# Chunked attention into a phase MLP on one core: the first group's q and k on SyncE's queue in fp32, theta on the load queue, and another written order

## The chip, the cores and the metric

The kernel runs on one NeuronCore of a Trainium2 chip. The metric is the device time of one execution in microseconds (us); smaller is better. The engines are named as in the profile: PE (TensorE; PEld is its weight load), DVE (VectorE), ACT (ScalarE), POOL (GpSimd) and SP (SyncE). POOL and SP issue DMAs, and so does ACT.

## The reference

Attention inside chunks of 64 tokens, for 8 batches, 8 heads, 576 tokens and a head width of 64; its output, with the heads side by side, is the input x (8 x 576 x 512) of an MLP layer:

```python
scores = scale * q_c @ k_c^T            # per chunk of 64, softmax over the chunk
x      = softmax(scores) @ v_c          # (B, S, 512)
theta  = x @ w_theta
y      = w_tok_r @ (x * cos(theta)) + w_tok_i @ (x * sin(theta))   # over tokens
u      = x + y
out    = u + max(u @ w_ch, 0)
```

All inputs and the output are fp32. The kernel works in fp16 with fp32 sums.

## The kernel before, in words

The 8 batches are worked off as 4 pairs (p = 0 to 3). The 1152 tokens of a pair are cut into five groups: A and B are 256 tokens each of the first batch, C and D of the second, and M holds the last 64 tokens of both. A step of the kernel is one stage for one group, and for some steps one half of it (the digit behind the letter).

Nothing is scheduled by a tool at run time: the text ORDER (line 16) lists every step, and the loop at the end emits them in that order (lines 769 to 782), so each engine executes its instructions in the order in which they stand there. A step is written `kind.pairgroup.bank`; `S1.0A.2` is the scores of the second half of group A of pair 0 into PSUM bank 2. The kinds that matter here are:

- `q`, `k` (line 173): load of a group's q or k by POOL's queue, which casts fp32 to fp16 on the way. It has two layouts. In the usual one two tokens lie in one partition, so that a packet reads 512 bytes; in the plain one (`qP`, `kP`) one token does, two DMAs are issued, and a packet reads 256 bytes. `v` (line 205) issues three DMAs for a group, two for M. `lw`, `lc` and `lt` load the weights; `lt` (line 240) brings theta in fp32 by SP's queue and `ctV` casts it on DVE.
- `L`, `T`, `N` (line 285): transposes of q and k on PE, in three forms. `T` (small) takes 64 transposes of 64x64 for a group, `L` (long) 32 of 64 to 128 wide, `N` (plain, needed for a plain load) 16 of 128x128. `tq`, `tkA`, `tkV` (line 328) copy the results out of PSUM, q by DVE and k by ACT or DVE.
- `S`, `e`, `V`, `n`: scores on PE, exp on ACT, product with v on PE, normalisation on DVE, which gives x.
- `X`/`Q`, `xA`/`xV`: transposes of x on PE (128x128, or small ones of 64x64) and their copy by ACT or DVE. `H`: product with theta (line 479), `g`: cos and sin on ACT, `z`: their products with x on DVE.
- `TW`, `twV`: transposes of the token weights and their copies. `Y`, `K`: the product over tokens (lines 551, 565, 654). Pair 0 takes it straight (`Y`); the pairs 1 to 3 take a form with fewer products (`K`), with sums of z (`j`) on DVE.
- `U`/`R`, `uA`/`uV`, `W`, `w`, `s`/`sA`: transposes of u, their copies, the product with w_ch, the relu and sum on DVE, and the store by SP's (`s`) or ACT's (`sA`) queue.
- `D.n`: n dummy matmuls of 128x512 on zeros (line 276), which need only the memset of `init` (line 131).

Three things hold loads back. For the pairs 1 to 3 a load step first copies one element of the newest normaliser on POOL (`gate`, line 167), so that POOL waits until DVE got there. The tiles of q, k, token weights, sums of z and the late outputs share one pool of ten buffers (`nat`, line 105), so that a load waits until the tile ten allocations earlier was read for the last time. And POOL's loads use eight semaphores in turn, so that the ninth waits for the first to land. PSUM's eight banks are given out by hand in ORDER.

Of the kernel before, what the change touches and what calls it, by code (L numbers as in the profile page):

```python
# [9 lines left out]
FP32 = mybir.dt.float32  # L10
FP16 = mybir.dt.float16
# [2 lines left out]


ORDER = """
lt.00 init.00 id.00 D.12.0 ctV1.00 q.0A k.0A D.19.0 L0.0A.0.1 tq0.0A q.0C L1.0A.2.3 tq1.0A k.0C
v.0A tkA1.0A S1.0A.2 L.0C.0.4 tq.0C tkA0.0A S0.0A.6 e1.0A tkA.0C q.0B k.0B e0.0A ctV0.00 D.3.0
V0.0A.0 V1.0A.2 n1.0A S.0C.6 e.0C q.0M n0.0A L0.0B.7.6 L1.0B.5.4 X0.0A.0 tkA0.0B tq0.0B k.0M
N1.0M.1 v.0B N0.0M.2 tq1.0B tkA1.0B S1.0B.6 tq1.0M tq0.0M X1.0A.3 xA0.0A e1.0B S0.0B.4 e0.0B  # L20
tkV1.0M S1.0M.0 e1.0M v.0C V1.0B.6 xV1.0A tkV0.0M n1.0B S0.0M.2 e0.0M V0.0B.4 n0.0B H0.0A.0
V0.0C.6 n0.0C pg.00 g0.0A V1.0C.2 v.0M X1.0B.1 xV1.0B H1.0A.4 q.0D g1.0A X0.0B.7 V0.0M.6 V1.0M.1
H1.0B.5 g1.0B n1.0C X.0C.0 xV0.0B k.0D L.0D.7.2 tkA.0D n0.0M n1.0M X.0M.1 z0.0A xV.0M lw.00
tq.0D z1.0A H0.0B.3 H.0M.1 S.0D.4 g0.0B xV.0C TW.01.6 TW.00.2 g.0M lw.02 e.0D twV.01 v.0D H.0C.0
q.1B twV.00 YA.0A.2 k.1B q.1A V0.0D.4 z1.0B z0.0B V1.0D.6 z.0M YB.0A.2 YM.0A.2 g.0C TW.02.0
n1.0D TW.03.6 twA.02 n0.0D Q.0D.4 y.0A T.1B.2 R.0A.0 lc.00 twV.03 YA.0B.6 xA.0D uA.0A jw.00
jw.01 H.0D.0 tkA.1B g.0D tq.1B z.0C k.1A S.1B.4 T.1A.2 tq.1A YM.0B.6 q.1D YB.0B.6 tkA.1A W.0A.0
q.2A k.2A T.2A.2 y.0B e.1B tkA.2A k.1D T.1D.6 tkA.1D z.0D YD.0C.4 tq.2A YC.0C.4 S.1A.2 q.1M e.1A
w.0A q.1C k.1C k.1M T.1C.0 v.1B tq.1D S.1D.6 tq.1C YM.0C.4 v.1C YD.0D.2 YM.0D.2 e.1D y.0C
V0.1B.4 tkA.1C lw.04 V1.1B.0 v.1A sA.0A n0.1B S.1C.6 e.1C n1.1B YC.0D.2 y.0D X.1B.0 TW.04.1  # L30
twV.04 N.1M.7 tq.1M xA.1B S.2A.4 e.2A V0.1A.2 v.1D v.1M q.3B V1.1A.0 Y.0M.6 n1.1A n0.1A tkA.1M
V0.1C.0 S.1M.2 y.0M e.1M k.3B V1.1C.4 n1.1C U.0D.7 X.1A.6 v.2A n0.1C uA.0D xV.1A H.1B.2 V0.1D.0
pg.00 g.1B V1.1D.4 n1.1D H.1A.6 q.2M V0.1M.5 g.1A n0.1D n0.1M V1.1M.4 n1.1M z.1B Q.1C.0 xA.1C
q.2C k.2C W.0D.2 U.0B.4 V0.2A.6 uA.0B w.0D v.2B X.1D.5 n0.2A H.1C.0 T.3B.6 V1.2A.2 xA.1D H.1D.4
q.2D z.1A g.1C g.1D tq.3B v.2D v.2M W.0B.0 n1.2A Ka.1A.2 v.3A z.1C tkA.3B Q.1M.4 ja.1C w.0B
T.2C.6 Q.2A.0 ra.1A xA.1M H.1M.4 U.0C.5 xA.2A tq.2C z.1D tkA.2C k.2M H.2A.0 g.1M q.2B k.2B jb.1D
Ke.1C.6 z.1M v.3B re.1D Kf.1C.2 rc.1C uA.0C W.0C.4 w.0C Kc.1D.6 T.2B.4 g.2A sA.0D jc.1D jd.1B
S.2C.0 pe.00 e.2C tq.2B tkA.2B rd.1C Kg.1D.2 rg.1B Kd.1B.0 rh.1B v.2C S.2B.4 e.2B q.3C Km.1D.2
U.1C.7 uA.1C S.3B.0 k.3C rf.1D V1.2C.4 k.2D Y.1M.6 T.2D.2 q.3M n1.2C e.3B sA.0C y.1M tkA.2D
V0.2C.0 n0.2C V1.2B.4 U.1B.7 uA.1B tq.2D N.2M.6 U.0M.0 uA.0M X.2C.1 xA.2C tq.2M Kb.1B.2 tkA.2M  # L40
S.2D.0 n1.2B s.0B V0.2B.4 z.2A W.1B.6 rb.1A n0.2B e.2D V0.2D.0 n0.2D S.2M.2 w.1B H.2C.4 V1.2D.0
e.2M v.3M W.0M.2 U.1A.3 n1.2D V0.2M.0 w.0M Q.2B.6 n0.2M V1.2M.1 n1.2M X.2D.2 pg.00 g.2C z.2C
W.1C.4 xA.2D w.1C H.2D.0 xA.2B uA.1A V0.3B.2 q.3A s.0M ja.2C n0.3B g.2D Q.2M.6 xV.2M H.2B.4 g.2B
R.1M.2 uV.1M V1.3B.0 T.3C.6 H.2M.2 g.2M U.1D.3 uA.1D n1.3B z.2D tq.3C jb.2D tkA.3C s.1B Ka.2A.0
s.1C k.3M ra.2A v.3C Ke.2C.4 jc.2D Q.3B.2 xA.3B S.3C.6 e.3C z.2M q.3D Kf.2C.0 rc.2C W.1D.2 k.3D
k.3A w.1D z.2B H.3B.6 pg.00 g.3B re.2D Kg.2D.0 rg.2B T.3D.2 tkA.3D W.1A.6 tq.3D v.3D Km.2D.0
w.1A Kc.2D.4 S.3D.2 rf.2D rd.2C pe.00 e.3D T.3A.0 Kb.2B.6 tq.3A jd.2B N.3M.2 rb.2A sA.1D tkA.3A
S.3A.0 tkA.3M V1.3D.4 Y.2M.3 tq.3M S.3M.6 n1.3D e.3A V0.3A.4 y.2M V0.3D.0 W.1M.2 U.2A.3 n0.3D
e.3M n0.3A uA.2A X.3D.0 xA.3D V0.3M.1 w.1M V1.3A.6 n1.3A Kd.2B.4 X.3A.0 n0.3M rh.2B V0.3C.6
V1.3M.1 H.3D.2 xA.3A n1.3M n0.3C Q.3M.0 pg.00 g.3D xV.3M V1.3C.4 n1.3C H.3A.6 z.3B Q.3C.0 xV.3C  # L50
R.2B.4 W.2A.2 z.3D w.2A g.3A z.3A uA.2B H.3M.0 H.3C.6 g.3M z.3M R.2D.0 g.3C R.2C.2 W.2B.4 z.3C
ja.3C Kb.3B.6 rb.3A jb.3D uA.2C W.2C.2 uA.2D w.2C sA.2A Ka.3A.6 ra.3A W.2D.0 Ke.3C.2 Kf.3C.6
sA.2C sA.1A w.2B re.3D jc.3D rc.3C Kc.3D.2 R.3A.4 Kg.3D.6 s.2B rd.3C uA.3A W.3A.2 jd.3B Kd.3B.4
rg.3B w.2D s.2D w.3A Km.3D.6 R.3C.0 uA.3C rh.3B Y.3M.2 rf.3D s.1M R.3B.0 uV.3B sA.3A R.3D.6
W.3C.4 y.3M uA.3D W.3D.6 w.3C U.3M.0 W.3B.4 w.3D uV.3M sA.3C w.3B R.2M.0 sA.3D s.3B W.3M.2 uA.2M
W.2M.0 w.3M sA.3M w.2M sA.2M
""".split()


# [1 line left out]
def kernel(  # L61
# [11 lines left out]
    nc = tc.nc  # L73
    B, H, S, D = q.shape
    DM = H * D
    CH = 64
    P = 128
    NDB = DM // P
    NE = H // 2
# [4 lines left out]
    GT = 2 * P  # L84
# [5 lines left out]
    GROUPS = {  # L90
        "M": (MID, None, KT * P),
        "A": (0, 0, 0),
        "B": (2, 0, GT),
        "C": (5, 1, 0),
        "D": (7, 1, GT),
    }
# [8 lines left out]
    nat = ctx.enter_context(tc.tile_pool(name="nat", bufs=10))  # L105
# [16 lines left out]
    wtheta16 = glob.tile([P, NDB, DM], FP16, name="wtheta16")  # L122
# [1 line left out]
    wT = glob.tile([P, NK, S], FP16, name="wT")  # L124
    wsum = [glob.tile([P, 2, 2, GT], FP16, name=f"wsum{i}") for i in range(4)]
    v16 = glob.tile([P, 2 * NT, H, VP], FP16, name="v16")
    wraw = []
    wnat = {}

    def setup():  # L130
# [9 lines left out]
    st = {p: {} for p in range(NP)}  # L140
# [23 lines left out]
    nats = {}  # L164
    marks = []

    def gate(p):

        if p and marks:
            nc.gpsimd.tensor_copy(out=seen, in_=marks.pop())  # L170
            marks.clear()

    def load_qk(p, g, which, plain, f=None):
# [28 lines left out]
            ),  # L202
        )

    def load_v(p, g):

        gate(p)
        j0, bb, s0 = GROUPS[g]
        slot = (p % 2) * NT + j0
        if bb is None:  # L210
            for b in range(2):
                nc.gpsimd.dma_start(
                    v16[half[b], slot, :, 0:D],
                    v[2 * p + b, :, s0 : s0 + CH, :].rearrange("h s d -> s h d"),
                )
            return
        for rows, tile, t0, m in (
            (slice(0, P), 0, s0, P),
            (half[1], 1, s0 + P, CH),
            (half[0], 1, s0 + P + CH, CH),  # L220
        ):
            nc.gpsimd.dma_start(  # L222
                v16[rows, slot + tile, :, 0:D],
                v[2 * p + bb, :, t0 : t0 + m, :].rearrange("h s d -> s h d"),
            )
# [12 lines left out]
                wnat.setdefault(i + j, []).append(t[:, j])  # L238

    def load_theta():  # L240
        for a in range(2):
            t = nat.tile([P, 2, DM], FP32, name="wraw", tag="nat")
            wraw.append(t)
            nc.sync.dma_start(
                t, moe_w_theta[a * GT : a * GT + GT, :].rearrange("(a p) e -> p a e", p=P)
            )

    def cast_theta(a, copy):
        copy(out=wtheta16[:, 2 * a : 2 * a + 2], in_=wraw[a])

    def load_w_ch():
        nc.gpsimd.dma_start(wch16, moe_w_ch.rearrange("(a p) e -> p a e", p=P))
# [75 lines left out]
    def qk_copy(p, g, f, which, how):  # L328
        ps = st[p]["ps_qkT", g, f][which]
        _, nx, n, c = ps.shape  # L330
        name = "qk"[which] + "T"
        t = tmp.tile([P, nx, n, c], FP16, name=name, tag=f"{name}{n}")
        st[p][name, g, f] = t
        if how == "V":
            nc.vector.tensor_copy(out=t, in_=ps)  # L335
        elif n == 1 or st[p]["form", g, f] == "plain":
            nc.scalar.copy(out=t, in_=ps)
        else:
            nc.scalar.copy(  # L339
                out=t.rearrange("p x s c -> p x (s c)").rearrange(  # L340
                    "p x (c s) -> p x c s", s=2
                ),
                in_=ps.rearrange("p x s c -> p x c s"),
            )
# [355 lines left out]
    def store(p, g, f, queue):  # L700
# [12 lines left out]

    work = {
        "v": load_v,
        "lt": lambda p, g: load_theta(),
        "id": lambda p, g: make_identity(nc, id16),
# [17 lines left out]
        "k": lambda p, g, f: load_qk(p, g, 1, False, f),  # L735
        "qP": lambda p, g, f: load_qk(p, g, 0, True, f),
        "kP": lambda p, g, f: load_qk(p, g, 1, True, f),
        "ctA": lambda p, g, f: cast_theta(f, nc.scalar.copy),
        "ctV": lambda p, g, f: cast_theta(f, nc.vector.tensor_copy),
        "T": lambda p, g, f, *banks: qk_t(p, g, f, "small", *banks),  # L740
        "L": lambda p, g, f, *banks: qk_t(p, g, f, "long", *banks),
        "N": lambda p, g, f, *banks: qk_t(p, g, f, "plain", *banks),
        "tq": lambda p, g, f: qk_copy(p, g, f, 0, "V"),
        "tkV": lambda p, g, f: qk_copy(p, g, f, 1, "V"),
        "tkA": lambda p, g, f: qk_copy(p, g, f, 1, "A"),
        "S": scores,
# [22 lines left out]
    with tc.manual_schedule():  # L769
        for step in ORDER:  # L770
# [5 lines left out]
            p, g = int(at[0]), int(at[1]) if at[1].isdigit() else at[1]  # L776
# [36 lines left out]
```

## Time and profile before

| what | value |
|---|---|
| three timed executions | 206.13, 206.96, 207.36 us; median 206.96 |
| the profiled execution, its own time | 207.38 us |
| its span in the trace | 205.5 us |
| PE busy | 190.5 us (93%) |
| DVE, ACT, POOL busy | 153.8, 118.1, 88.5 us |
| mean granted PE clock | 0.981 |
| bytes moved by DMA packets | 26.99 MB, 16.01 of them by POOL's queue |

The profile is taken from one execution. The span runs from the program's first to its last instruction. Busy time counts what an engine executes, and for PE it includes the dummies. The table of windows gives the same busy times for stretches of the span, with the granted clock and the DMA traffic in each. The chain of waits starts at the last instruction and goes back, at each step, to what released it. A line of the groups shows the kind, the shapes, how often it ran, its busy time in us and its mean in ns.

### The profile page before, as it was taken

To read this page: it belongs to the slowest core of one execution; us is meant where nothing else is said; L and a number is where in the kernel's file an instruction comes from. 1 tells how busy PE (TensorE), PEld (TensorE's weight loads), DVE (VectorE), ACT (ScalarE), POOL (GpSimd) and SP (SyncE) were. 2 spreads that over 40 slices of the span, in tenths; PEclk is the share of its full clock that TensorE was granted. 3 is DMA by queue.
4 is the path that set the end of the run, shared out by engine and by line. 5 is a ranking of instruction groups with operands and counts; after the bars stand their busy time and mean duration, and the time that the engine had idled before them with its cause. 6 is when DMAs were issued, how large, how long until landed. Compare 5 with 4: busy or idle time off the path is not lost.

```text
span 205.5 us, 7697 instructions
## 1 busy us (share of the span) xinstructions
PE 190.5 (93%) x3472; PEld 102.5 (50%) x3472; DVE 153.8 (75%) x246; ACT 118.1 (57%) x139; POOL 88.5 (43%) x129
## 2 busy tenths in 40 slices
PE   7975999999669999999799999999999999999990
PEld 2454565464444755454456455454566444444540
DVE  0144678895436879997877898989988998799670
ACT  2065769778516598877157588888446983010310
POOL 8959983297761968889530040870000000000000
PEclk9999589999999999999999999999999999999998
DMA  6999999999993999999993059999200011613456
GB/s 210 170 171 149 103 186 178 192 162 174 167 129 111 82 151 88 166 200 200 157 168 113 3 55 197 142 134 99 100 5 3 3 38 69 243 67 115 143 219 189
DMA packets 86832, 26.99 MB, mean 131 GB/s; under 512 B 80016, under 2 KB 81680, under 8 KB 86800
## 3 DMA queue, kind: packets, MB, share of 16 engines
q0 software_dynamic: 81264, 16.01, 92.9%
q10 hardware_dynamic: 3040, 5.77, 7.9%
q1 hardware_dynamic: 2496, 4.72, 6.7%
q8 instruction: 27, 0.44, 0.9%
q14 instruction: 5, 0.04, 0.1%
HBM read 33.06 MB, written 9.44 MB: 207 GB/s over the span
## 4 chain that ended last, share of the span: by engine, by line
PE 80%; DMA 11%; POOL 3%; issue 2%; DVE 0%; POOLq 0%; DVEq 0%
PE ps L479 30%; PE ps L654 18%; PE ps L565 8%; DMA qk<-in_k_dram 7%; PE ps L439 5%; DMA v<-in_v_dram 4%; PE ps L551 4%; PE ps L401 3%; PE ps L319 3%; PE ps L367 3%; PE ps L448 3%; POOL qk L198 2%; PE ps L267 2%; PE ps L302 1%; POOL qk L184 1%
## 5 line engine op out<-in xcount | busy, mean ns | idle before, releaser
L222 POOL DMA_DIRECT2D v<-in_v_dram x48 | 36.4, 779 | 4.4 <-DMA qk<-in_k_dram 1.7
L479 PE MATMUL ps<-wtheta,xT 128*128 128x512 f16 x144 | 35.8, 390 | 0.0
L479 PE MATMUL ps<-wch,uT 128*128 128x512 f16 x144 | 34.1, 380 | 0.0
L673 DVE TENSOR_TENSOR x<-ps,x 128x1024 f16<-128x1024 f32 x24 | 29.1, 1222 | 5.7 <-PE ps L654 5.1
L462 ACT COPY uT<-ps 128x1024 f16<-128x1024 f16 (+1 forms) x17 | 16.2, 968 | 25.0 <-PE ps L448 17.5
L383 ACT ACTIVATE eT<-ps 128x1024 f16<-128x1024 f32 (+1 forms) x18 | 16.6, 930 | 19.0 <-PE ps L367 19.0
L415 DVE TENSOR_TENSOR x<-ps,recip 128x512 f16<-128x512 f32 (+1 forms) x40 | 25.5, 638 | 1.4
L339 ACT COPY kT<-ps 128x1024 f16<-128x1024 f16 (+1 forms) x18 | 16.4, 921 | 16.4 <-PE ps L306 11.9
L335 DVE COPY qT<-ps 128x1024 f16<-128x1024 f16 (+2 forms) x23 | 13.0, 572 | 16.5 <-PE ps L306 5.9
L493 ACT ACTIVATE cos<-ps,pihalf 128x1024 f16<-128x1024 f32 (+1 forms) x22 | 21.1, 959 | 7.3 <-PE ps L479 7.2
L694 DVE SCALAR_TENSOR_TENSOR o<-ps,x 128x1024 f32<-128x1024 f32 (+1 forms) x20 | 22.2, 1114 | 3.2 <-PE ps L479 2.6
L479 PEld LDWEIGHTS <-uT 128*128 128x128 f16 x144 | 13.3, 98 | 14.8 <-ACT uT L462 0.3
L479 PEld LDWEIGHTS <-xT 128*128 128x128 f16 x144 | 13.3, 100 | 14.3 <-issue 1.1
L497 ACT ACTIVATE sin<-ps 128x1024 f16<-128x1024 f32 (+1 forms) x22 | 19.0, 862 | 0.0
L654 PE MATMUL ps<-z,wT 128*128 128x512 f16 x72 | 18.8, 379 | 0.0
L170 POOL COPY seen<-recip 1x1 f32<-1x1 f32 x12 | 2.2, 181 | 34.0 <-DVE recip L413 34.0
L565 PE MATMUL ps<-z,wT 128*128 128x512 f16 x72 | 16.7, 380 | 0.0
L654 PE MATMUL ps<-zsum,wsum 128*128 128x512 f16 x72 | 16.7, 379 | 0.0
L198 POOL DMA_DIRECT2D qk<-in_q_dram x16 | 14.5, 909 | 3.2 <-issue 1.2
L462 ACT COPY xT<-ps 128x1024 f16<-128x1024 f16 (+1 forms) x13 | 12.3, 951 | 5.8 <-PE ps L439 3.4
L198 POOL DMA_DIRECT2D qk<-in_k_dram x16 | 14.4, 903 | 1.5 <-DMA qk<-in_k_dram 1.2
L654 PEld LDWEIGHTS <-wsum 128*128 128x128 f16 x96 | 9.2, 98 | 10.7
(66 smaller groups left out, 279.3 us busy)
## 6 DMA issues: line engine op xcount, KB each, us to landing
out_dram<-o ACTq DMA_DIRECT2D x10, 512.0 KB, 3.0
qk<-in_q_dram POOLq DMA_DIRECT2D x16, 256.0 KB, 6.5
qk<-in_k_dram POOLq DMA_DIRECT2D x16, 256.0 KB, 6.9
out_dram<-o SPq DMA_DIRECT2D x6, 512.0 KB, 4.2
v<-in_v_dram POOLq DMA_DIRECT2D x40, 64.0 KB, 5.4
v<-in_v_dram POOLq DMA_DIRECT2D x16, 128.0 KB, 6.4
wraw<-in_moe_w_theta_dram SPq DMA_DIRECT2D x2, 512.0 KB, 3.9
wnat<-in_moe_w_tok_r_dram POOLq DMA_DIRECT2D x2, 288.0 KB, 7.2
```

What stands on the lines that cost most here:

```text
L198: nc.gpsimd.dma_start(t.rearrange("p (h x) -> p h x", h=H)[:, hs], ap[2 * p + bb, :, s0 : s0 + GT, :].rearrange("h (p s) d -> p h (s d)", ...
L222: nc.gpsimd.dma_start(v16[rows, slot + tile, :, 0:D], v[2 * p + bb, :, t0 : t0 + m, :].rearrange("h s d -> s h d"),)
L383: nc.scalar.activation(out=eT.rearrange("p h r e c -> p (h r e) c"), in_=ps, func=AF.Exp, scale=scale)
L415: nc.vector.tensor_tensor(out=tokens(p, g, "x")[:, :, f * NE * D : (f + 1) * NE * D].rearrange("p c (h d) -> p c h d", h=NE), in0=psv[:, 0 ...
L462: (nc.vector.tensor_copy if how == "V" else nc.scalar.copy)(out=to.rearrange("p b (r c) -> p b r c", c=CH), in_=psv)
L479: nc.tensor.matmul(ps[:, a * DM : a * DM + cols.stop - cols.start], xT[:, b0 + a, db, :], weight[:, db, cols], start=(db == 0), stop=(db = ...
L493: nc.scalar.activation(out=cos[:, 0:n].rearrange("p a e -> p (a e)"), in_=pin, func=AF.Sin, bias=pihalf, scale=1.0,)
L497: nc.scalar.activation(out=sin[:, 0:n].rearrange("p a e -> p (a e)"), in_=pin, func=AF.Sin)
L565: nc.tensor.matmul(ps[:, a * DM : a * DM + DM], wT[:, kt, t0 : t0 + P], zs[bb], start=(done + k == 0), stop=(done + k == NK - 1),)
L654: nc.tensor.matmul(ps[:, a * DM : a * DM + DM], wt, zt, start=fresh and i == 0, stop=i == len(terms) - 1, skip_group_check=to in ("x", "z"),)
L673: nc.vector.tensor_tensor(out=u, in0=st[p]["ps_k", frm], in1=u, op=ALU.add)
L694: nc.vector.scalar_tensor_tensor(out=o, in0=ps[:, 0 : n * m].rearrange("p (j d) -> p j d", j=n), scalar=0.0, in1=u, op0=ALU.max, op1=ALU.add,)
```

## The change

SP no longer loads theta. It loads q and k of group B of pair 0 instead, each in two halves of four heads, uncast, into fp32 tiles (`hq`, `hk`); DVE and ACT cast two halves each (`cqV`, `ckV`, `cqA`, `ckA`). Theta goes through POOL's queue as one casting DMA, and its two casts on DVE go. `tqA` (a copy of q by ACT) exists but is not used. The rest is a new ORDER of 585 steps instead of 580. In it pair 0 begins with group B, then M, C, A and D; 5 of the 16 large groups load plain and use `N`, 6 use `L`, 5 use `T` (before: none, 4 and 12, where the halves of a group count as one); the dummies are `D.24`, `D.8`, `D.12` and `D.6` instead of `D.12`, `D.19` and `D.3`; some copies of x and u change between ACT and DVE, and the stores are 8 on SP and 8 on ACT among the large ones, instead of 6 and 10. Two table loads of ACT go (10 instead of 12). The sums, products and scores are as many as before.

In the built program DVE's first two instructions are the casts `cqV1` and `ckV0`, ahead of the memset of zeros; ACT's are a table load and the casts `cqA0` and `ckA1`; POOL's first loads are q and k of M, then A and C of pair 0.

```diff
 ORDER = """
-lt.00 init.00 id.00 D.12.0 ctV1.00 q.0A k.0A D.19.0 L0.0A.0.1 tq0.0A q.0C L1.0A.2.3 tq1.0A k.0C
-v.0A tkA1.0A S1.0A.2 L.0C.0.4 tq.0C tkA0.0A S0.0A.6 e1.0A tkA.0C q.0B k.0B e0.0A ctV0.00 D.3.0
-V0.0A.0 V1.0A.2 n1.0A S.0C.6 e.0C q.0M n0.0A L0.0B.7.6 L1.0B.5.4 X0.0A.0 tkA0.0B tq0.0B k.0M
...
+hq0.0B id.00 hq1.0B cqV1.0B cqA0.0B hk0.0B ckV0.0B hk1.0B q.0M ckA1.0B init.00 k.0M D.24.0
+L0.0B.0.1 tkA0.0B q.0A L1.0B.7.6 tq0.0B D.8.0 N0.0M.0 tkA0.0M S0.0B.4 N1.0M.1 tkA1.0M tq0.0M
+tq1.0M S1.0M.0 D.12.2 S0.0M.2 tkA1.0B e0.0B qP.0C tq1.0B S1.0B.4 kP.0C N.0C.6.7 tq.0C e1.0B v.0B
+k.0A e1.0M V0.0B.0 v.0M tkA.0C e0.0M S.0C.6 V1.0B.4 e.0C L0.0A.2.3 n1.0B n0.0B L1.0A.7.6 tq1.0A
+V0.0M.4 X1.0B.5 X0.0B.0 tq0.0A n0.0M tkA1.0A V1.0M.1 n1.0M S1.0A.6 xA1.0B tkA0.0A S0.0A.4 lt.00
+e0.0A X.0M.1 e1.0A xA0.0B H1.0B.2 g1.0B xA.0M v.0A V0.0A.6 V1.0A.4 q.0D n0.0A n1.0A z1.0B D.6.0
...
+    raw = {}
+
+    def load_first(p, g, which, f):
+
+        j0, bb, s0 = GROUPS[g]
+        if f not in raw:
+            raw[f] = nat.tile([P, 2, DM], FP32, name="raw", tag="nat")
+        nc.sync.dma_start(
+            raw[f][:, which].rearrange("p (h x) -> p h x", h=NE),
+            (q, k)[which][2 * p + bb, f * NE : f * NE + NE, s0 : s0 + GT, :].rearrange(
+                "h (p s) d -> p h (s d)", s=2
+            ),
+        )
+
+    def cast_first(p, g, which, f, copy):
+        if (p, g) not in nats:
+            nats[p, g] = nat.tile([P, 2, 2 * DM], FP16, name="qk16", tag="nat")
+        copy(out=nats[p, g][:, which, f * DM : f * DM + DM], in_=raw[f][:, which])
...
     def load_theta():
-        for a in range(2):
-            t = nat.tile([P, 2, DM], FP32, name="wraw", tag="nat")
-            wraw.append(t)
-            nc.sync.dma_start(
-                t, moe_w_theta[a * GT : a * GT + GT, :].rearrange("(a p) e -> p a e", p=P)
-            )
-
-    def cast_theta(a, copy):
-        copy(out=wtheta16[:, 2 * a : 2 * a + 2], in_=wraw[a])
+        nc.gpsimd.dma_start(wtheta16, moe_w_theta.rearrange("(a p) e -> p a e", p=P))
...
-        elif n == 1 or st[p]["form", g, f] == "plain":
+        elif which == 0 or n == 1 or st[p]["form", g, f] == "plain":
             nc.scalar.copy(out=t, in_=ps)
```

## The prediction

> **What bounds the kernel now.** I read the page first, then the table of windows, then the timeline of the first 36 us and the chain of waits.
>
> ```profile
> span 205.5 us, 7697 instructions
> PE 190.5 (93%) x3472; PEld 102.5 (50%) x3472; DVE 153.8 (75%) x246; ACT 118.1 (57%) x139; POOL 88.5 (43%) x129
> PEclk9999589999999999999999999999999999999998
> ```
>
> PE is busy for 93% and the granted clock dips once, near 20 us. Dummy matmuls (L278, 34 of them, 10.2 us) are part of the 190.5, so real work is 180.3 us. The windows show where the other 25 us are (columns: window, its length, busy time and count of PE, PEld, DVE, ACT, POOL, granted clock, DMA share, GB/s):
>
> ```profile
> 10.00:15.00 5.00, 4.04 (x102) 2.64 (x100) 2.14 (x4) 2.91 (x5) 2.58 (x5) 1.00 2.02 171
> 15.00:20.00 5.00, 2.42 (x102) 2.01 (x102) 2.51 (x6) 2.42 (x5) 4.50 (x7) 1.00 2.33 155
> 20.00:25.00 5.00, 4.85 (x94) 2.74 (x94) 3.11 (x9) 3.71 (x7) 4.50 (x7) 0.51 1.54 94
> 25.00:30.00 5.00, 5.00 (x93) 3.40 (x94) 4.16 (x12) 3.25 (x6) 4.31 (x7) 0.81 1.43 184
> 50.00:55.00 5.00, 3.44 (x139) 2.03 (x137) 2.42 (x3) 2.70 (x3) 3.51 (x5) 1.00 2.04 172
> 120.00:130.00 10.00, 10.00 (x232) 5.89 (x230) 8.97 (x18) 8.59 (x10) 2.05 (x5) 1.00 0.86 171
> ```
>
> PE starves at 15 to 20 us and at 50 to 60, while the DMA engines move 140 to 170 GB/s. After the first hunger the clock is at half: 5 us x 0.49 + 5 us x 0.19 = 3.4 us lost. From 60 us on PE is full, with 1.1 us idle near 100. The first stage in the timeline:
>
> ```profile
> 1.20 9.44 PE L278 MATMUL ps<-zeros 128*128 128x512 f16 x31 [1.20 <-DVE pihalf L132]
> 5.86 0.15 PEld L278 LDWEIGHTS <-zeros 128*128 128x128 f16 x1 [0.28 <-issue]
> 6.29 3.85 PEld L278 LDWEIGHTS <-zeros 128*128 128x128 f16 x18 [0.28 <-issue]
> 10.56 1.08 PE L306 MATMUL ps<-id,qk 128*64 128x128 f16 x32
> ```
>
> The dummies start 1.20 us in, run 0.43 us apart until 6.29 and 0.21 us apart after. Real work starts at 10.56, right behind them. In the chain the stalls have these names:
>
> ```profile
> 13.81 6.15 DMA qk<-in_k_dram
> 29.51 1.01 PE ps L306 x32
> 42.35 0.56 PE ps L319 x64
> 52.51 1.56 issue
> 67.80 0.55 PE ps L302 x8
> 92.95 8.08 DMA qk<-in_k_dram
> ```
>
> So the bound is PE's own work, plus a late start, plus hunger for loads up to 60 us. PE's idle time after 10.56, summed over the groups of PE, is 8.4 us (attention 0.5, scores 2.7, the three forms of q/k transposes 2.7, 2.1 and 0.3, dummies 0.1).
>
> **The change part by part.**
>
> *Start of PE.* Group 0B's q and k come as four fp32 half loads on SP (256 KB each). Before, SP's two 512 KB loads were issued at 0.74 and 1.24 and landed 3.25 and 4.53 us later (timeline, landings), so 512 KB moves in 1.8 us. Four halves, issued 0.45 apart, land near 3.3, 4.1, 4.9 and 5.7. In the built program the first two instructions of DVE are casts of these loads; the memset of zeros stands behind them, and the 24 dummies at the head of PE wait for that memset. Casts: no row for 128x512 from fp32; the 128x1024 cast took 0.69, a 128x512 copy 0.42, so I take 0.42. Third load 4.9, cast 0.42, two memsets 0.33: dummies from 5.7 instead of 1.20. If the slow spell is again 5.1 us (12 dummies), the other 12 take 12 x 0.214 = 2.6 and PE starts real work at **13.4**, though its data are cast by 6.5. Against 10.56 that is **+2.8**. Bounds: all 24 at the fast spacing (5.1 us) gives 10.8, all at the slow one (10.3 us) 16.0.
>
> The trace has the fast spacing after 5.1 us of dummies. The Trainium skill (TensorE: Matmul & The Clock Gate, Part 1) says that the clock opens after one busy window of some 3.4 us of a free-running counter, so the slow spell would be 3.4 to 6.8 us by phase; the one spell in this trace lies in between. By that rule the start would be 12.6 to 14.2.
>
> *q/k transposes.* Before: 12 whole groups in the small form (64 transposes of 64x64), four group equivalents in the long form (32), none in the plain form (16 of 128x128). After: 5, 6 and 5. Costs by the chain: 64 of the small form 0.56 to 0.64, I take 0.58; 32 long 1.01; 16 plain 2 x 0.45, the 0.55 of the line above being the upper end. Before 12 x 0.58 + 4 x 1.01 = 11.0; after 5 x 0.58 + 6 x 1.01 + 5 x 0.90 = 13.5. **+2.5** us, most of it where PE has no idle time (bounds 1.9 and 3.3). Transposes of x: 12 more of 128x128 at 0.055, 48 fewer of 64x64 at 0.01: **+0.2**.
>
> *Dummies inside.* 3 before, 8 + 12 + 6 = 26 after, all in the first stage: 23 x 0.216 = **+5.0**. They cost nothing only where PE would have waited anyway; that is counted in the idle time below.
>
> *Clock.* With the dummies PE is busy for about 85% of each 3 us after its start, not 48% as at 15 to 20; I let the dip go: **-3.4** (bounds 0 and -3.4).
>
> *Loads.* POOL loses 1 MB (fp32) of 0B and gains 1 MB of theta, which goes in longer packets: about nothing. Five groups load plain, two DMAs of 128-byte packets for one of 256-byte packets. In the trace's packet records 256-byte packets ran at some 700 a us and 128-byte ones at 1150: 2048/1150 = 1.8 us for 1024/700 = 1.45, +0.3 a load, +0.6 a group, 1.9 by 60 us. POOL's own issue grows by 0.9 us a load, 1.8 for 1.8 of transfer, so it barely keeps up; the bound from the issue side is 5 us by 60 us. Whether PE meets it: at 150 to 170 GB/s from 4.6 us (when the first packets of the queue moved), theta, with 1.7 MB ahead of it, lands at 18 to 20; PE wants it at 13.4 + 10.6 (sum of its steps) + 1.5 = 25.5. k of 1C, 6.9 MB into the queue, lands at 45 to 50; PE wants it near 53.8. The loads are 4 to 6 us ahead, so the hunger of before goes, because PE is late and has 26 dummies, not because loads are early.
>
> *Idle time after.* What is late next is ACT: its kT copies (0.59 and 1.02), exps (0.60, 1.02), xT copies and a table load (1.28) fill the 10 us from PE's start to the first product with theta. Setting each PE step behind its copy: the scores of M wait 0.4, those of C 0.85 (1.02 less one attention half), later scores of A 0.3, the turn of A 0.2, the product of A behind the Sin table 0.5. That is 2.2; I add 1.0 for the rest of the span (before: 1.4 after 65 us). 3.2 instead of 8.4: **-5.2** (bounds -7.5 and -2).
>
> *At no cost.* DVE: two casts of 0.69 become two of 0.42 and copies change sides, +0.9 of 153.8. ACT loses two table loads (2.6) and gains two casts (1.2). Both are hidden behind PE; DVE at 9 of 10 us from 70 to 190 is the thinner cover, and without it these come in full. The stores move between queues; they end as before with group 2M on ACT's queue, so the 5.4 us behind PE's last matmul stay.
>
> **Sum:** +2.8 +2.5 +0.2 +5.0 -3.4 -5.2 = **+1.9** on the profiled execution's 207.38: 209.3. That execution is 0.4 above the median of its runs (206.96), so I forecast **208.9**.
>
> **The rivals.**
> 1. *Forecast*: late start, more PE work, no hunger. Own range 207.2 to 210.6 (start 12.6 to 14.2, idle 2.3 to 4.1). Chance 0.50.
> 2. *Faster: PE waits for nothing any more.* Place: 13 to 60 us. If the new order lets ACT's copies finish under the dummies, idle time falls to 0.8 and the start comes at 12.6: +1.9 - 2.4 - 0.8 = -1.3, 205.7 (204.4 to 207). The turning point is an idle time of 1.3 us with the start at 13.4. For: 10 us of ACT's work lie against 10.6 of PE's in the first stage, so a slightly better interleaving hides it. Against: ACT was busy for 9.2 of 10 us at 30 to 40 already. Chance 0.32.
> 3. *The clock falls again.* If the steps between dummies are too thin, half a clock for 6.8 us returns: +3.4, 212.3. For: before, the window of 10 to 15 us was 81% busy and the dip came one window later. Against: 26 dummies. Chance 0.08.
> 4. *The narrow packets bind.* If POOL's issue sets the pace (5 us by 60), k of 1C and 1D come 1 to 3 us too late for PE: +2, 210.9. For: 94 GB/s at 20 to 25 us, when v's short DMAs were issued at 0.7 us each. Chance 0.10.
> That the early q and k bring no early start (their use waits for 24 dummies) is part of the forecast.
>
> **How the numbers follow.** About 0.5% (1.0 us) is what a measurement can tell from no change: below 205.9 and above 208.0. Rival 2 gives 0.22 below 205.9 and 0.10 within; the forecast gives 0.14 within and 0.36 above; 3 and 4 lie above. Faster 0.22, same 0.24, slower 0.54. The range 204.9 to 211.5 leaves out about 0.08 below, and rival 3 with a sliver of 4 above, 0.1.
>
> **What would show it.** Right: PE's first transposes at 12.6 to 14.2; first dummies behind DVE's casts near 5.7; a granted clock of 1.00 from there on; PE idle 2 to 4 us after its start; no PE wait for a load before 60 us; the first product with theta near 25.5. Wrong: transposes before 12 us, a start of theta's product before 24, or PE idle under 1.3 us in all (faster); a clock under 0.9 in any window after 13 us, or scores and transposes waiting for DMA between 40 and 65 (slower still).

## The result and the profile after

| | before | after |
|---|---|---|
| median of the timed executions | 206.55 us (4: 205.53 to 207.36) | 212.70 us (4: 212.18 to 213.09) |
| ratio after / before, 95% interval | | 1.0299 (1.0244 to 1.0354) |
| the profiled execution, its own time | 207.38 us | 212.77 us |
| its span, mean granted PE clock | 205.5 us, 0.981 | 210.3 us, 0.999 |

The ratios, here and for the runs below, compare only the executions that fall into the faster of two states that a kernel shows, so they can differ from the quotient of the medians, which take in all.

The change makes the kernel slower by 3%. The sign is that of the forecast; the size is not: 212.7 lies 1.2 us above the top of the range (211.5).

The page of the kernel after:

```profile
span 210.3 us, 7073 instructions
PE 194.3 (92%) x3148; PEld 104.6 (50%) x3148; DVE 154.4 (73%) x244; ACT 113.7 (54%) x141; POOL 96.5 (46%) x139
PEclk9999999999999999999999999999999999999999
```

The dip of the clock is gone, and PE is 3.8 us busier than before. The table of windows, after (columns as in the prediction):

```profile
5.00:10.00 5.00, 2.46 (x6) 0.89 (x7) 1.32 (x5) 0.72 (x2) 5.00 (x7) 1.00 1.82 190
10.00:15.00 5.00, 5.00 (x21) 1.96 (x21) 0.00 (x0) 0.00 (x0) 4.33 (x7) 1.00 2.34 157
15.00:20.00 5.00, 4.21 (x75) 2.79 (x75) 1.34 (x4) 2.23 (x5) 4.87 (x7) 1.00 1.70 183
20.00:25.00 5.00, 4.20 (x88) 2.46 (x89) 0.69 (x1) 2.18 (x5) 3.21 (x6) 1.00 2.06 171
50.00:55.00 5.00, 5.00 (x37) 2.75 (x36) 1.90 (x5) 2.40 (x3) 4.86 (x8) 1.00 2.06 171
```

At 50 to 55 us PE is now full where before it worked for 3.44 of 5 us: the hunger for loads is gone. But from 10 to 15 us 19 of PE's 21 instructions are dummies (the other two are the first transposes, at 14.97), while DVE and ACT do nothing at all. The chain of waits, after (start, length, what), says what put the dummies there:

```profile
1.24 0.50 SPq L212
1.78 4.98 DMA raw<-in_k_dram
6.79 0.43 DVE qk L222
7.22 0.27 DVE zeros L131
7.54 7.49 PE ps L289 x24
15.04 1.01 PE ps L317 x32
```

The path starts with SP's third half load, which lands 4.98 us after its issue; then DVE casts it, DVE clears the zeros, and only then can PE start its 24 dummies. The timeline, after, dates the steps that the prediction named:

```profile
7.54 7.49 PE L289 MATMUL ps<-zeros 128*128 128x512 f16 x24 [7.54 <-DVE pihalf L132]
14.97 1.08 PE L317 MATMUL ps<-id,qk 128*64 128x128 f16 x32
29.45 1.03 PE L490 MATMUL ps<-wtheta,xT 128*128 128x512 f16 x4
```

The dummies start at 7.54 instead of 1.20, the first transposes at 14.97 instead of 10.56 (forecast 13.4), and the first product with theta at 29.45 (forecast 25.5). PE's waits from 10 to 120 us, after, hold no load:

```profile
PE ps L378 <- ACT kT L348: 0.8, 1, 0.8
PE ps L378 <- DVE qT L346: 0.8, 1, 0.8
PE ps L378 <- ACT kT L350: 0.6, 1, 0.6
PE ps L317 <- ACT eT L394: 0.4, 1, 0.4
PE ps L450 <- DVE x L426: 0.2, 1, 0.2
```

The only other wait that the view lists for the whole span is the 7.5 us ahead of the first dummy. The landings show why: theta landed at 20.53 and is used at 29.45, k of 0A at 17.41 for 25.35, the last v of 0A at 22.36 for 30.53, the last v of 0B at 16.34 for 23.72. The last half load of 0B itself landed at 8.12, 6.8 us ahead of the first transposes.

### The profile page after: what moved, and what is told of

It is laid out like the page before. It is cut to its first block, busy times and chain, and to the rows that moved or that the text cites. A ratio compares the mean times of both kernels' runs of the same rounds, so it can differ in the third digit from the quotient of the medians.

```text
span 210.3 us, 7073 instructions
## 1 busy us (share of the span) xinstructions
PE 194.3 (92%) x3148; PEld 104.6 (50%) x3148; DVE 154.4 (73%) x244; ACT 113.7 (54%) x141; POOL 96.5 (46%) x139
## 4 chain that ended last, share of the span: by engine, by line
PE 89%; DVE 2%; ACT 2%; DMA 2%; SPq 0%; issue 0%; DVEq 0%; ACTq 0%
PE ps L490 30%; PE ps L665 20%; PE ps L576 8%; PE ps L289 6%; PE ps L450 4%; PE ps L562 4%; PE ps L313 3%; PE ps L378 3%; PE ps L412 3%; PE ps L459 3%; DMA raw<-in_k_dram 2%; PE ps L317 2%; PE ps L278 1%; PE ps L330 1%; DVE x L426 1%; ACT eT L394 1%
## 5 line engine op out<-in xcount | busy, mean ns | idle before, releaser
L490 PE MATMUL ps<-wtheta,xT 128*128 128x512 f16 x144 | 34.6, 380 | 0.0
L473 ACT COPY uT<-ps 128x1024 f16<-128x1024 f16 (+1 forms) x16 | 14.5, 906 | 29.2 <-PE ps L459 24.8
L426 DVE TENSOR_TENSOR x<-ps,recip 128x512 f16<-128x512 f32 (+1 forms) x40 | 25.5, 638 | 1.4
L346 DVE COPY qT<-ps 128x1024 f16<-128x1024 f16 (+2 forms) x23 | 12.9, 569 | 14.6 <-PE ps L317 7.3
L350 ACT COPY kT<-ps 128x1024 f16<-128x1024 f16 (+1 forms) x13 | 11.4, 888 | 18.6 <-PE ps L317 11.8
L289 PE MATMUL ps<-zeros 128*128 128x512 f16 x50 | 13.6, 431 | 7.6 <-DVE pihalf L132 7.5
L473 ACT COPY xT<-ps 128x1024 f16<-128x1024 f16 (+1 forms) x16 | 13.1, 831 | 6.5 <-PE ps L450 4.3
L424 DVE RECIPROCAL recip<-ps 128x8 f32<-128x8 f32 (+1 forms) x40 | 7.9, 198 | 9.3 <-PE ps L412 7.0
L170 POOL COPY seen<-recip 1x1 f32<-1x1 f32 x13 | 3.1, 236 | 25.3 <-DVE recip L424 25.3
```

The source lines that it names most:

```text
L289: nc.tensor.matmul(psum(bank, 1), zeros[:, 0:P], zeros)
L426: nc.vector.tensor_tensor(out=tokens(p, g, "x")[:, :, f * NE * D : (f + 1) * NE * D].rearrange("p c (h d) -> p c h d", h=NE), in0=psv[:, 0 ...
L473: (nc.vector.tensor_copy if how == "V" else nc.scalar.copy)(out=to.rearrange("p b (r c) -> p b r c", c=CH), in_=psv)
L490: nc.tensor.matmul(ps[:, a * DM : a * DM + cols.stop - cols.start], xT[:, b0 + a, db, :], weight[:, db, cols], start=(db == 0), stop=(db = ...
```

## The experiments

Runs 1 to 6 and 9 turn on one question: is the late start the loss, one for one, or do other parts of the change (the inner dummies, the forms, the fp32 path) carry it? The others price single parts. Each run has its own runs of the kernel before on the same chip (medians 206.0 to 206.2). The times are medians; spans and stages are those of the profiled execution.

**1. The memset ahead of the casts.** The step `init.00` moves to the head of ORDER; nothing else changes.

```diff
-hq0.0B id.00 hq1.0B cqV1.0B cqA0.0B hk0.0B ckV0.0B hk1.0B q.0M ckA1.0B init.00 k.0M D.24.0
+init.00 hq0.0B id.00 hq1.0B cqV1.0B cqA0.0B hk0.0B ckV0.0B hk1.0B q.0M ckA1.0B k.0M D.24.0
```

> The changed kernel with one edit: the memset of zeros stands ahead of the casts on DVE, so the first 24 dummies start near 1.2 us instead of 7.54. Theory A (the loss is a PE that starts late while its loads already wait): the first transposes start at 8.8 to 9.2 us instead of 14.97, and since every load of the first stage landed 8 us or more ahead of its use (theta 20.5 against 29.5, k of 0A 17.4 against 25.4, v of 0A 22.4 against 30.5), nearly all of the 6 us comes off the end: 206.5 to 207.5 us, the same as before within 0.5%. Rival B (ACT's copies and exps or the loads hold the first stage): the start moves, but the first product with theta stays at 27 us or later and the time stays above 209.5.

Measured: 206.68 us, ratio to before 1.0026 (0.9995 to 1.0056), 6.0 us less than after and in theory A's range. Its timeline:

```profile
1.19 8.06 PE L289 MATMUL ps<-zeros 128*128 128x512 f16 x24 [1.19 <-DVE pihalf L132]
9.18 1.08 PE L317 MATMUL ps<-id,qk 128*64 128x128 f16 x32
23.66 1.03 PE L490 MATMUL ps<-wtheta,xT 128*128 128x512 f16 x4
```

The transposes come 5.8 us earlier, theta's product 5.8 us earlier, and the time falls by 6.0. PE's idle time behind its start is the same 3.14 us. So every microsecond of the late start goes to the end, and moving one step of ORDER takes the whole loss back: with it the change is as fast as the kernel before.

**2. Without the inner dummies.** `D.8.0`, `D.12.2` and `D.6.0` go; the 24 at the head stay.

```diff
-... tq0.0B D.8.0 N0.0M.0 ... S1.0M.0 D.12.2 S0.0M.2 ... z1.0B D.6.0
+... tq0.0B N0.0M.0 ... S1.0M.0 S0.0M.2 ... z1.0B
```

> The changed kernel without the dummies D.8, D.12 and D.6; the 24 at the head stay. They take 5.7 us of PE. Theory A: 2.5 to 4.5 us come off (208.2 to 210.2), the rest turns into waits for ACT's kT copies and exps; the granted clock stays at 1.00. Rival C (they keep the clock up): the clock falls to half for a stretch of 6.8 us between 20 and 35, and the time stays at 212 or more.

Measured: 211.75 us, ratio 1.028 (1.020 to 1.036), 1 us less than after instead of 2.5 to 4.5. All dummies together take 5.9 us less. Of that 2.7 us came back as idle time and 1.5 as longer rows at a half clock later on; another 0.8 is that the dummies at the head began at 8.38 instead of 7.54 in this execution. The half clock in its windows:

```profile
25.00:30.00 5.00, 4.59 (x98) 2.76 (x98) 1.22 (x4) 4.02 (x7) 2.48 (x4) 0.66 1.40 200
```

The time lies between the two ranges: theory A's gain is missed, and C's fall of the clock happened (0.66) but did not quite outweigh the dummies. The 26 dummies nearly pay for themselves, and are not where the 6 us went.

**3. Both edits together.**

> Both edits: memset first, and no dummies after the first 24. Theory A: the gains add until the loads are met: first transposes near 9, first product with theta at 21 to 22.5 (theta lands near 20.5), 203 to 205.5 us, which is faster than before. Rival B: no more than the better of the two edits alone, 206 or above. Rival C: half clock in a stretch after 13 us, 206 to 208.

Measured: 205.70 us, ratio 0.9999 (0.9964 to 1.0034); only 1.0 us less than with the memset alone, just above the 203 to 205.5 of theory A. Now the loads are met: theta's product starts at 22.6 right behind theta's landing at 21.8, PE waits (up to 30 us) 1.5 us for a q or k and 0.5 for v, and the clock falls, as rival C had it:

```profile
15.00:20.00 5.00, 4.38 (x107) 3.52 (x109) 1.84 (x5) 2.32 (x3) 4.42 (x6) 0.52 1.68 181
```

**4. The transposes back in the small form.** The groups 0C, 1A, 1B, 1D, 2A, 2C, 2D and 3D of the kernel after take `T` with plain loads turned back to usual ones.

```diff
-TW.04.2 uA.0B N.1A.0.1 tq.1A ...
+TW.04.2 uA.0B T.1A.0 tq.1A ...
-L.2D.3.2 tq.2D L.2A.0.1 tkA.2D ...
+T.2D.2 tq.2D T.2A.0 tkA.2D ...
```

> The changed kernel with eight whole groups (0C, 1A, 1B, 1D, 2A, 2C, 2D, 3D) loaded and transposed as before, in the small form (64 transposes of 64x64) with one DMA per load. Theory A (PE is the bound, so its added work counts in full): qk transposes fall by 8 x (0.95 - 0.60) = 2.8 us at most and 1.7 at least, 210.0 to 211.2. Rival (the added PE work lies in waits that exist anyway): 212 or above. The start stays at 15.0 in both.

Measured: 222.76 us, ratio 1.080 (1.070 to 1.089), 10 us slower than after. Theory A is wrong about it, and the rival's 212 or above holds in number only: it said that the longer form hides in waits, not that the small form adds new ones. PE's transposes did get shorter, by 1.5 us (16.05 to 14.6 in the rows of the three forms), but its idle time went from 3.1 to 11.0, and its other rows of real work grew by 2.7 us, with the clock at half for 3.4 us from 25.1 and from 103.6. One such wait, near 103 us, in the timeline of this kernel:

```profile
103.69 1.01 PE L450 MATMUL ps<-id,x 128*128 128x128 f16 x8 [2.74 <-DVE qT L346]
```

A turn of u waits for DVE's copy of q of 2A out of PSUM, though ACT's copy of k had ended at 100.9; in the kernel after, the same turn follows the scores at 97.92 without a wait. The small form puts q and k side by side in both of its banks, so neither is free until both copies are done; the long form frees one bank with each copy. The written order had planned its banks on that. So the longer transposes were no loss that could be had back alone; this wait shows that they pay for PSUM. For the other 5.2 us of idle time that was not traced wait by wait.

**5. The fp32 path in the old order.** Before's ORDER, with q and k of 0A by SP in halves and cast, the memset first, and theta by POOL behind v of 0B.

```diff
-lt.00 init.00 id.00 D.12.0 ctV1.00 q.0A k.0A D.19.0 L0.0A.0.1 ...
+init.00 hq0.0A id.00 hk0.0A hq1.0A hk1.0A D.12.0 cqA0.0A ckV0.0A cqV1.0A ckA1.0A D.12.0 L0.0A.0.1 ...
-N1.0M.1 v.0B N0.0M.2 ...
+N1.0M.1 v.0B lt.00 N0.0M.2 ...
```

> The load path of the change alone, in the order of before: q and k of group 0A in fp32 halves by SP, cast by ACT and DVE, theta by POOL behind v of 0B; memset first, 24 dummies at the head. Theory A (early q and k help once PE may start): first transposes near 9.0 us instead of 10.56, M's q and k land some 3 us earlier than 20.0, so the hunger at 15 to 20 us and the dip of the clock shrink: 1.5 to 4 us faster than before, 202.5 to 205. Rival D (the queue moves the same bytes, so the waits only move to a later load): within 0.5% of before.

Measured: 207.85 us, ratio 1.0143 (1.0063 to 1.0223): slower than before, which neither had. The first transposes come 1.5 us earlier (9.09), and nothing is gained: theta is now late, as its wait shows,

```profile
PE ps L489 <- DMA wtheta<-in_moe_w_theta_dram: 1.1, 1, 1.1
```

the second half of 0A waits 0.8 for its cast, and PE's idle time stays at 7.9 us. In the old order PE meets its loads, and here an early start only waited longer.

**6. The new order without the fp32 path.** After's ORDER, with q and k of 0B first in POOL's queue, theta in fp32 by SP and cast by DVE as before, and the memset at once.

```diff
-hq0.0B id.00 hq1.0B cqV1.0B cqA0.0B hk0.0B ckV0.0B hk1.0B q.0M ckA1.0B init.00 k.0M D.24.0
+lt.00 init.00 id.00 ctV1.00 ctV0.00 q.0B k.0B q.0M k.0M D.24.0
```

> The new order alone: q and k of 0B first on POOL's queue, theta in fp32 by SP with its two casts on DVE, memset at once. Theory A (the loss was the memset behind the casts, and the rest of the order is about as good as before's): first transposes near 9.2 us, the first product with theta 0.5 to 1.5 us later than the 23.7 of the kernel with the memset first, 206.5 to 208.5. Rival E (the order is worse by itself and the fp32 path makes up for it): 209 or more.

Measured: 206.74 us, ratio 1.0078 (1.0049 to 1.0108), in theory A's range, with transposes at 9.39, theta's product at 24.26 and 3.2 us of idle time. Against run 1 (206.68, ratio 1.0026) the fp32 path by itself is worth nothing by the medians and about 1 us by the ratios, whose intervals overlap: behind the 24 dummies PE waits only 0.2 us for a load of 0B. The path's cost came through the memset behind its casts.

**7. Eight dummies where run 3 starved.** Run 3 with `D.8.2` ahead of `N.0C`.

> Memset first, no D.8, D.12, D.6, but 8 dummies just ahead of the transposes of 0C, where PE waited for loads until 15 us. Theory A: the dip of the clock (15 to 22 us, 3.2 us of extra busy time against the kernel without it) goes, idle time stays near 4 us: 203 to 204.5, faster than before by 1% or more. Rival C (dummies cost what they save): 205.5 or above.

Measured: 206.52 us (204.62 to 209.97), ratio 1.0026 (0.9983 to 1.0068). The profiled execution, 204.62 at a clock of 0.996, is the fastest of ten and just above theory A's range; the others are 1.0 to 5.4 us slower. By the median the run falls to rival C (205.5 or above), and the interval leaves no room for a gain of 1%. Whether the eight dummies gain or lose a little against run 3 (ratio 0.9999) it does not decide, since the executions differ among themselves by more.

**8. Dummies in the gaps of before.** `D.6.4` ahead of `L0.0B` and `D.6.3` ahead of `N1.0M`, to take the dip of the clock out of the kernel before.

```diff
-... q.0M n0.0A L0.0B.7.6 ...
-N1.0M.1 v.0B ...
+... q.0M n0.0A D.6.4 L0.0B.7.6 ...
+D.6.3 N1.0M.1 v.0B ...
```

> The kernel before with 6 dummies ahead of the transposes of 0B and 6 ahead of those of M, where PE waits for loads at 16 to 17 and 18 to 19 us. It prices the dip of the clock (20.1 to 26.9 us), which the prediction took at 3.4 us. If 3.4 is right: 203 to 204.5, less what the dummies overrun. If the dip costs about 2 us, as the busy times of products with theta and of transposes say: 204.5 to 206. If the clock was not a loss: 206.5 to 207.5.

Measured: 208.15 us, ratio 1.0135 (1.0045 to 1.0224), slower than any of the expectations. The dip is gone. The windows of before,

```profile
20.00:30.00 10.00, 9.85 (x186) 6.13 (x188) 7.26 (x21) 6.96 (x13) 8.81 (x13) 0.66 1.48 139
45.00:60.00 15.00, 12.00 (x283) 6.18 (x281) 7.87 (x11) 7.53 (x8) 11.79 (x17) 1.00 1.93 161
```

and of this kernel:

```profile
20.00:30.00 10.00, 9.43 (x211) 6.01 (x210) 7.11 (x22) 7.47 (x15) 9.76 (x15) 1.00 1.46 132
45.00:60.00 15.00, 11.18 (x267) 5.76 (x266) 7.13 (x10) 7.27 (x7) 11.03 (x16) 1.00 1.94 164
```

The clock at 20 to 30 us rises from 0.66 to 1.00, and from 45 to 60 PE is idle for 3.8 us instead of 3.0, at the same 160 GB/s. PE's rows of real work fall by some 2 us; the idle time rises from 8.4 to 9.3 and the dummies by 1.7 (the 12 new ones take 2.7, those at the head 1.0 less). The first product with theta starts at 23.22 in both kernels. So taking the dip out brought the end nothing, which fits that the loads of before set the pace up to 60 us. Why this kernel is even slower than before is not shown.

**9. The memset between the two casts.** `init.00` stands between `cqV1` and `ckV0`, so that it waits for the second half load, not the third.

```diff
-... cqV1.0B cqA0.0B hk0.0B ckV0.0B hk1.0B q.0M ckA1.0B init.00 k.0M D.24.0
+... cqV1.0B cqA0.0B init.00 hk0.0B ckV0.0B hk1.0B q.0M ckA1.0B k.0M D.24.0
```

> The changed kernel with the memset between DVE's two casts, so the dummies start at 5.8 us, which is the start that the prediction assumed (5.7), instead of 7.54; first transposes at 13.3 (prediction 13.4) instead of 14.97. If the late start goes to the end one for one: 1.7 us off the changed kernel, 210.4 to 211.4. So the prediction's 208.9 would still be missed by about 2 us, and that part belongs to its other terms. If the end does not follow the start in this range: 212 or more.

Measured: 210.79 us, ratio 1.0192 (1.0129 to 1.0255), in the range of the late start that goes to the end one for one. Its timeline:

```profile
5.76 8.21 PE L289 MATMUL ps<-zeros 128*128 128x512 f16 x24 [5.76 <-DVE pihalf L132]
```

The dummies start at the 5.7 that the prediction had assumed, and the transposes at 13.90 (13.3 was expected), 1.07 earlier than after; the span is 1.1 us shorter. Even then the time is 1.9 us above the forecast of 208.9: the start is not the only mis-sized term.

**10. A late start in the old order.** Before, with `D.31` for `D.19`: 12 dummies more ahead of the same work.

> The kernel before with 12 more dummies at its head (D.31 for D.19): PE's first transposes come 2.6 us later, near 13. Theory F (before 60 us that kernel waits for its loads, so a late start costs nothing there): 206 to 207, within 0.5% of before. Theory G (a late start goes to the end in either kernel): 208 to 209.

Measured: 208.17 us (205.56 to 210.14), ratio 1.0056 (1.0006 to 1.0106). The median lies in theory G's range, the ratio (207.3 us) between the two. For 2.6 us of dummies the interval gives 0.1 to 2.2 us, so in the old order a late start is hidden at least in part; how far is not settled.

**11. The long form in the old order.** Before, with `L` for `T` in seven groups (2B, 2C, 2D, 3A to 3D), where PE is full.

> The kernel before with seven late groups (2B, 2C, 2D, 3A to 3D) transposed in the long form (32 transposes of 64x128) instead of the small one, in the same banks; loads as before. It prices the form where PE has no idle time (after 65 us). If each group costs 0.95 instead of 0.60: 7 x 0.35 = 2.5 us slower, 208 to 209. If PE's waits take it up: 206 to 207.

Measured: 207.72 us, ratio 1.0096 (1.0061 to 1.0130), that is 2.0 us by the ratio and 1.5 by the medians, between the two expectations. The group of the long form grew from 128 to 352 instructions:

```profile
L306 PE MATMUL ps<-id,qk 128*64 128x128 f16 x352 | 12.1, 220 | 1.9 <-ACT eT L383 1.2 <-issue 0.7
```

By the times between starts PE's rows gained 7.1 and lost 4.3 us, 0.40 a group (the prediction's 1.01 less 0.58 is 0.43). So of 2.8 us of added work about two thirds reach the end here (by the interval 1.3 to 2.7 us).

**12. Dummies in two gaps.** The memset first, `D.8.0` and `D.12.2` out, `D.8.2` ahead of `N.0C`, `D.6.0` kept.

> Memset first; dummies only where PE waited: 8 ahead of the transposes of 0C and 6 at their old place ahead of the turn of A. Against the kernel with the 8 alone: if the second gap (1.5 us of waits at 23 to 25) is free, the same 206 or up to 1 us less, because the clock dips less often: 204.8 to 206.2. If they push the products with theta out: 206.5 to 207.5.

Measured: 205.18 us, ratio 0.9944 (0.9905 to 0.9982), in the range of a free second gap. It is the only kernel of the study that is faster than before, by 0.6%. Its largest wait of PE is now a load:

```profile
PE ps L412 <- DMA v<-in_v_dram: 1.9, 3, 1.3
```

**13. POOL's queue later.** The kernel after, in which POOL first fills an unused tile three times, so that its packets do not lie beside SP's half loads.

```diff
-hq0.0B id.00 hq1.0B ...
+pd.00 hq0.0B id.00 hq1.0B ...
+        "pd": lambda p, g, f: [nc.gpsimd.memset(idle, 0.0) for _ in range(3)],
```

> The kernel after, in which POOL first fills an unused tile three times (128x1536), so that its load queue begins some microseconds later and POOL's narrow packets do not lie beside SP's four fp32 half loads. Which part of the computation is left out: none. Theory P (the third half load is late because it shares the DMA engines with POOL's 128-byte packets): it lands 3.0 to 3.6 us after its issue, as the first two did (4.8 to 5.5 us into the span, 6.76 in the kernel after), the dummies start at 5.6 to 6.3 instead of 7.54, PE's first transposes come 1.3 to 1.9 us earlier, and, if PE still waits for no load (they were 8 us ahead), the whole takes 210.8 to 211.6. Rival Q (SP's queue needs that time by itself, whatever POOL does): the third half load again lands 4.5 to 5.2 us after its issue, the dummies start at 7.2 to 7.9, and the time is 212 to 213. If the later queue makes PE wait for a load, an idle time over 4 us in the span would show it, and only the landing and the dummies' start count.

Measured: 211.73 us, ratio 1.0264 (1.0189 to 1.0338); the profiled execution 211.97 instead of 212.77. The timeline of this kernel, POOL, DVE and PE:

```profile
5.72 1.50 POOL L185 DMA_DIRECT2D qk<-in_q_dram  x2
5.81 0.43 DVE L223 CAST qk<-raw 128x512 f16<-128x512 f32 x1 [0.54 <-DMA raw<-in_k_dram]
6.56 7.90 PE L290 MATMUL ps<-zeros 128*128 128x512 f16 x24 [6.56 <-DVE pihalf L133]
```

The four half loads land at 3.74, 4.59, 5.78 and 6.54; in the kernel after it was 3.78, 4.70, 6.76 and 8.12. So the third lands 4.0 us after its issue instead of 4.98: between P and Q. About half of its delay over the 3.1 that the prediction took is SP's own queue, the other half POOL's packets beside it. The dummies start 0.98 us earlier, but their slow part is longer this time (24 take 7.90 instead of 7.49), so the transposes gain 0.58 and the span 0.7.

## Why the prediction was wrong in size

Term by term, on the profiled executions (after less before, in us). The rows of PE count the time from each start to the next start or its own end:

| term | forecast | measured |
|---|---|---|
| start of PE | +2.8 | +4.4 |
| dummies inside | +5.0 | +4.9 |
| transposes of q and k | +2.5 | +1.6 (small -4.28, long +1.82, plain +4.10) |
| transposes of x | +0.2 | +0.1 |
| clock | -3.4 | -1.9 (theta's products -1.43, scores -0.48) |
| other rows of PE | 0 | +1.0 (w_ch +0.64, the mix of tokens +0.3, others) |
| idle time of PE | -5.2 | -5.3 (8.41 to 3.14) |
| behind PE and outside the span | 0 | +0.5 |
| sum | +1.9 | +5.4 |

What held: the memset stands behind the casts and pushes the start; the early q and k bring no early start; the loads are ahead and the hunger does not come back; the granted clock is 1.00; PE's idle time is what ACT's copies and exps and DVE's copies leave. Run 1 confirms the mechanism alone, in one line. The idle time's total (3.1 for 3.2) is right partly by luck: the scores of M wait 0.8 instead of 0.4 and those of A 0.6 instead of 0.3, and A's second transposes 0.4 that had no term, while the Sin table costs nothing instead of 0.5 and the rest of the span 0.1 or so instead of 1.0.

Which steps failed:

- **Start, 1.6 us too small.** The step "Four halves, issued 0.45 apart, land near 3.3, 4.1, 4.9 and 5.7" was scaled by bytes from theta's loads, which had 2 KB packets. The half loads have 512-byte packets, and POOL's queue starts beside them at 3.6 us. The packet records of after show 430 to 570 of SP's packets a microsecond until about 4 us and 270 to 440 beside POOL's. Run 13 splits the 1.86 us by which the third load came after its forecast of 4.9: it lands at 5.78 without POOL (0.9 of it), 6.76 with it (1.0). The 24 dummies themselves took 7.49 us for the 7.7 forecast.
- **Clock, 1.5 us too large.** The step "5 us x 0.49 + 5 us x 0.19 = 3.4 us lost" charged the lost clock to all of PE's time. The rows fell by only 1.9; run 8, which takes the dip out of before, finds 2.0 in all rows but the dummies'. And it gave that kernel's end nothing. Before's own executions agree: of the 59 that the ratios of the runs use, the 14 with a mean granted clock of 0.990 or more have a median of 205.7 us, the 7 below 0.980 one of 205.4. The loss belonged to the same stretch as the idle time that the next term took off.
- **Other rows, 1.0, and the rest, 0.5.** The products with w_ch and the mix of tokens took a little longer in the new order, for which the prediction had no term: of the products with w_ch 10 instead of 3 have 0.31 us to the next start, the others 0.22 in both kernels. Why is open. The time outside the span is 2.5 us in after, 2.4 in run 1 and 1.7 to 2.1 in the profiled executions of the runs 4, 5, 6 and 8; what sets it is open.
- **The correction of 0.4** for a profiled execution above its median did not carry over: that of after lies 0.1 above its median.

The transposes of q and k went the other way, 0.9 too large, as the small form costs more than 0.58 a group in before's rows (4.28 for seven groups, 0.61) and the others less (the long form 0.91, the plain one 0.82).

The first product with theta came 4.0 us later than forecast. The start is 1.6 of that; the steps between took 11.8 us instead of the prediction's 10.6, and the waits 2.7 instead of 1.5. The total of the idle time hides the longer waits, since the rest of the span has fewer.

Of the rivals none occurred. The clock did not fall, no load bound PE, and the idle time did not go below 3.1; the price above the forecast came from terms of the forecast that were mis-sized and, for 1.5 us, from time that had no term. The prediction's own bounds for the start, 10.8 to 16.0, did hold the 14.97; but the forecast's range went on with 12.6 to 14.2, which varies the dummies' pace alone and takes the landing of the third half load as known, though no row of before showed such a load.

The warm-up's pace is the part that varies from run to run. The slow spell was 5.1 us in before and 4.25 in after, and the 24 dummies took 7.49, 7.90, 8.06 and 8.21 in after and the runs 13, 1 and 9. The Trainium skill (TensorE: Matmul & The Clock Gate, Part 1) says that the clock opens after a whole busy window of 3.4 us of a free-running counter, from which 3.4 to 6.8 us by phase is an estimate. Both traces lie inside it; over all runs the spell goes from 3.3 us (run 8), just under it, to 5.95 (run 6).

The Trainium skill (TensorE: Matmul & The Clock Gate, HAM oscillation) has the rule that PE must not idle for more than some 3.4 us at a stretch. In the trace of before the clock falls without such a stretch: its longest gap between 10 and 20 us is 1.17 us, PE works for 2.42 of the 5 us from 15 to 20, and the clock falls to half at 20.1.

## What to carry to other kernels

DVE took its instructions in the written order: the memset of 0.27 us ran at 7.22 behind the casts, at 0.86 ahead of them (run 1). So an instruction that others wait for at the start goes ahead of the first one that waits for a DMA; behind it, it cost 6 us. Whether a late start costs anything is read from the landings: with every load some 7 us early or more it cost one for one (runs 1 and 9), where PE meets its loads it was partly hidden (run 10), and there an earlier start or a higher clock brought nothing (runs 5 and 8). A form of transposes is also a plan for PSUM: the dearer one may be what lets the next product start (run 4).

## What the runs showed of the hardware

- A load's landing depended on its place, its packets and its neighbours more than on its size: 512 KB in 2 KB packets landed 3.25 us after issue as the first of its queue (before); 256 KB in 512-byte packets landed 3.0 us after issue as the first, 4.0 as the third (run 13), and 5.0 as the third beside POOL's 128-byte packets (after; 5.3 to 5.8 in the runs 1, 2, 3 and 9).
- Dummies that keep the clock up can cost as much as they save: 12 of them in before (run 8) raised the clock from 0.66 to 1.00 in 10 us, and the kernel became 1.35% slower (0.45 to 2.2).
- Executions of one kernel can differ by more than some of the changes studied: those of before beside the runs have spans of 201.9 to 207.5 us at mean clocks of 0.967 to 0.999, and run 7 ranges from 204.62 to 209.97, while the ten executions of run 1, like the ten of run 6, lie within 1.3 us.
